# Attention and a gated spectral filter in one kernel: one load per ScalarE table, an earlier idle burst, split gates, and new orders for every engine

## The chip, the cores and the metric

One core of a Trainium2 chip runs the program. The metric is the device time of one execution in microseconds; lower is better. The engines are TensorE (PE), ScalarE (ACT), VectorE (DVE), GpSimd (POOL) and SyncE (SP, which issues most transfers). The profile gives starts and durations of the instructions of one execution.

## The reference

Eight batches, twelve heads, 448 positions, 64 elements to a head; float32 in and out.

```python
scores = scale * np.matmul(q, k.transpose(0, 1, 3, 2))
m = np.max(scores, axis=-1, keepdims=True)
e = np.exp(scores - m)
attn = e / (np.sum(e, axis=-1, keepdims=True) + np.exp(-m) + 1e-09)
x = np.matmul(attn, v)                     # then heads side by side: (8, 448, 768)
proj = x @ w_proj                          # 768 x 2304
x1, x2, x3 = proj[..., :D], proj[..., D:2*D], proj[..., 2*D:]
x2_conv = irfft(rfft(x2, axis=1) * rfft(filter_fft, axis=0))
out = (x1 * x2_conv * x3) @ w_out
```

## The kernel before, in words

Matrices are multiplied in bf16. The work of a batch has two parts.

**Attention** runs over six pairs of heads. For each pair the keys and queries are loaded, cast to bf16 and turned so that the head's elements lie across the partitions. PE makes four score tiles (`S`, t = 0 to 3; tile 0 holds the last 64 keys of both heads), ACT takes the exponential of each (`exps`, lines 852 and 858), PE multiplies by the values (`V`, line 878, with a column of ones that gives the sum), and DVE divides (`norm`). The result is turned again (`X`, line 975 for batch 0, by transfers for the others).

**The dense part** folds the turned result into even and odd parts along the sequence (`first`, `second`), projects it (`P`, line 1067, or `PS`, line 1089), takes the spectrum by matmuls with sines (`Z`), multiplies by the filter's spectrum on DVE, goes back (`I`), makes two gates (`G`, line 1189: six matmuls over the 768 inputs, `part` 0 copied by ACT, `part` 1 multiplied by it on DVE), and projects to the output (`O`, line 1003). Attention of the next batches is mixed with the dense part of the earlier ones on every engine.

**What sets the order.** Each step is given to a planner by `add(engine, cost, want, emit, need, make, take, give)`. `need` and `make` are the step's dependencies, `take` and `give` its buffers and PSUM banks. The tuple `plan.ORDER` has one rank for each `add` call, in the order of the calls; each engine emits its own steps strictly by rank. The planner also plays the steps through with the written costs, to choose PSUM banks and to put idle matmuls (line 1464) into gaps on PE near the start. An engine executes its steps in the written order and waits in place for what a step needs; SP's and POOL's transfers stand in the same queues as their other steps.

**The start.** `idle` is a zeroed tile and `spin` (line 1472) multiplies it 38 times, a burst of idle matmuls. `phases` and `sines` build the table of sines (DVE, then ACT at line 707); two one-column activations, `warm` with Exp (line 1479) and `warm` with Sin (line 1477), have no use but that of loading a function table. The compiler puts an ACT_TABLE_LOAD ahead of any activation whose function isn't in the table that is loaded. `staged(b)` loads batches 0 and 1 in float32 (`sk`, `sq`, `sv` for keys, queries, values of a pair; `rk`, `rv` for the last 64 positions), casts them (`ck`, `cq`, `cv`; pair 0's keys and queries on DVE, the rest on POOL) and turns them on PE (`T`, lines 530 to 539); later batches are turned by transposing transfers on SP. The weights come by POOL's queue: the filter, then w(0), w(1,0), w(1,1), w(2) and the output weights; w(1,0) and w(1,1) are the halves of the middle third of `w_proj`, which `P` uses.

**The end.** A check for very small denominators is read as a branch; the last output projections stand behind it.

## Time and profile before

| | us |
|---|---|
| median of 3 runs | 380.03 (379.71 to 380.31) |
| the profiled execution | 377.33 |
| its span, first to last instruction | 375.3 |
| PE busy, of the span | 358.9 |
| ACT, DVE, POOL busy | 265.3, 260.5, 113.8 |

The profiled execution is one execution, with a time of its own: its span and 2.0 us around it. Busy times are sums over one engine's instructions. In lists of instructions the columns are start, duration, engine, line, operation, output and inputs, count; in brackets stands how long the engine had been idle, and what ended that.

### The profile page before, as it was taken

The numbers are of one execution on the slowest core, as the hardware profiler recorded it, in microseconds if no ns is written. First come the engines' busy times: TensorE is split into PE (matmuls) and PEld (weight loads), VectorE is DVE, ScalarE is ACT, GpSimd is POOL, SyncE is SP. The second block draws the span as 40 slices with busy tenths as digits, with TensorE's granted clock in tenths as the row PEclk, the third lists the DMA queues.
The fourth block names the chain that finished last, engine by engine and source line by source line (L and its number), as shares of the span: only waits on it lengthen the run. The fifth ranks groups of instructions, "written<-read, shape, count | busy, mean of one in ns | idle before, by whom it ended". The sixth has DMA issues, their size and how long they took to land. (4 is left out here: it accounts for less than half of the span.)

```text
span 375.3 us, 9304 instructions
## 1 busy us (share of the span) xinstructions
PE 358.9 (96%) x3586; PEld 215.8 (58%) x3586; DVE 260.5 (69%) x676; ACT 265.3 (71%) x457; POOL 113.8 (30%) x240
## 2 busy tenths in 40 slices
PE   4899999999999999999899999999999999999985
PEld 4567675656665575555455556655555556555543
DVE  6389488865898556994498848684576936958570
ACT  5899967786877677677489477777788766436523
POOL 5765735142555441733272443120000000000000
PEclk9999999999999999999999999999999999999999
DMA  8999999999999999999999889796713054513304
GB/s 224 270 247 239 248 245 192 215 196 248 252 216 228 241 259 216 271 230 234 245 232 250 193 188 226 191 184 165 113 16 86 2 75 137 128 15 72 127 7 169
DMA packets 132019, 68.41 MB, mean 182 GB/s; under 512 B 88765, under 2 KB 128384, under 8 KB 131968
## 3 DMA queue, kind: packets, MB, share of 16 engines
q1 hardware_dynamic: 127248, 62.11, 73.6%
q0 software_dynamic: 4480, 5.41, 8.5%
q8 instruction: 29, 0.48, 0.5%
q10 hardware_dynamic: 240, 0.23, 0.2%
q14 instruction: 22, 0.18, 0.1%
HBM read 43.86 MB, written 11.01 MB: 146 GB/s over the span
## 5 line engine op out<-in xcount | busy, mean ns | idle before, releaser
L852 ACT ACTIVATE e<-psum 128x896 bf16<-128x896 f32 x144 | 126.8, 923 | 20.3 <-PE psum L839 18.0
L1189 PE MATMUL psum<-xT,wproj_bf 128*128 128x448 bf16 x576 | 121.8, 352 | 0.3 <-DVE kT L549 0.2
L1189 PEld LDWEIGHTS <-wproj_bf 128*128 128x128 bf16 x576 | 53.2, 97 | 46.4 <-issue 3.4
L1003 PE MATMUL psum<-wout_bf,yT 128*128 128x384 bf16 x288 | 52.8, 326 | 0.0
L878 PE MATMUL psum<-vn,e 128*128 128x65 bf16 x1152 | 46.9, 194 | 0.0
L878 PEld LDWEIGHTS <-e 128*128 128x128 bf16 x1152 | 41.6, 98 | 5.1 <-issue 0.8
L839 PE MATMUL psum<-qT,kT 64*128 64x448 bf16 x288 | 41.5, 355 | 1.4 <-DMA kT<-nat 0.9
L1157 DVE TENSOR_TENSOR t<-xs,hrs 113x768 bf16<-113x768 bf16 (+1 forms) x64 | 39.6, 641 | 4.3 <-ACT xs L1151 4.1
L1204 DVE TENSOR_TENSOR g<-x,psum 128x448 bf16<-128x448 bf16 x48 | 29.5, 615 | 17.3 <-PE psum L1189 14.2
L636 POOL CAST nat<-nat 112x512 bf16<-112x512 f32 x36 | 23.7, 666 | 49.6 <-DMA nat<-in_q_dram 47.6
L1089 PE MATMUL psum<-xf,wproj_bf 128*128 128x452 bf16 x180 | 38.6, 356 | 0.0
L1303 ACT COPY osb<-psum 128x384 f32<-128x384 f32 x56 | 25.5, 487 | 18.3 <-PE psum L1003 11.4
L1003 PEld LDWEIGHTS <-yT 128*128 128x128 bf16 x288 | 27.3, 98 | 18.6 <-issue 1.1
L1151 ACT CAST xs<-psum 113x384 bf16<-113x384 f32 (+1 forms) x64 | 29.0, 488 | 12.3 <-PE psum L1139 8.3
L1201 ACT CAST x<-psum 128x448 bf16<-128x448 f32 x48 | 25.7, 539 | 14.5 <-PE psum L1189 13.8
L893 DVE TENSOR_TENSOR xb<-psum,den 128x512 bf16<-128x512 f32 x48 | 33.2, 691 | 1.7
L858 ACT ACTIVATE er<-psum 128x448 bf16<-128x448 f32 x48 | 26.2, 549 | 11.2 <-PE psum L841 10.9
L1237 ACT CAST cr<-psum 128x452 bf16<-128x452 f32 x48 | 24.6, 545 | 7.9 <-PE psum L1228 5.8
L668 POOL CAST vn<-nat 128x192 bf16<-128x192 f32 x58 | 22.6, 416 | 24.9 <-PE psum L878 14.8
L891 DVE TENSOR_SCALAR den<-psum 128x8 f32<-128x8 f32 x48 | 7.8, 163 | 31.7 <-PE psum L878 26.4
L656 POOL CAST nat<-nat 128x384 bf16<-128x384 f32 x29 | 17.1, 594 | 32.5 <-DMA nat<-in_k_dram 31.6
L1067 PE MATMUL psum<-wproj_bf,xf 128*113 128x384 bf16 x144 | 26.6, 328 | 0.0
(130 smaller groups left out, 464.6 us busy)
## 6 DMA issues: line engine op xcount, KB each, us to landing
nat<-in_q_dram SPq DMA_DIRECT2D x47, 224.0 KB, 4.3
out_dram<-osb SPq DMA_DIRECT2D x24, 384.0 KB, 3.3
nat<-in_v_dram SPq DMA_DIRECT2D x41, 192.0 KB, 4.4
nat<-in_k_dram SPq DMA_DIRECT2D x41, 192.0 KB, 4.3
wproj_bf<-in_moe_w_proj_dram POOLq DMA_DIRECT2D x2, 1152.0 KB, 12.6
rests<-in_k_dram SPq DMA_DIRECT2D x8, 192.0 KB, 5.3
rests<-in_v_dram SPq DMA_DIRECT2D x8, 192.0 KB, 4.9
out_dram<-osb SPq DMA_DIRECT2D x8, 192.0 KB, 3.0
```

What stands on the lines that cost most here:

```text
L839: nc.tensor.matmul(sc[:, u, 0:S], kT[b % 2][c, hp, t, :], qT[b % 2][c, hp, :])
L852: nc.scalar.activation(to, of, AF.Exp, scale=SCALE)
L858: nc.scalar.activation(to, of, AF.Exp, scale=SCALE)
L878: nc.tensor.matmul(out_bank(u)[:, n, :], P["e"][1 + t][:, u * S + n * 128 : u * S + n * 128 + 128], vn[b % 2][:, hp, 4 * u + t, :], start= ...
L893: nc.vector.tensor_tensor(W["xb", b][:, hp].rearrange("p n (u d) -> p u n d", u=2), op[:, :, :, 0:DH], rec[:].unsqueeze(3).to_broadcast([1 ...
L1003: nc.tensor.matmul(ops[:n, :DCH], y[:, dt, 0:n], wout_bf[:, dt, ch * DCH : (ch + 1) * DCH], start=(dt == 0), stop=(dt == NDT - 1),)
L1067: nc.tensor.matmul(pps[:FQ, :DCH], W["xf", b][:, pg, kt, 0:FQ], wproj_bf[:, kt, D + ch * DCH : D + (ch + 1) * DCH], start=(kt == 0), stop= ...
L1089: nc.tensor.matmul(pps, wproj_bf[:, kt, D + dt * 128 : D + (dt + 1) * 128], W["xf", b][:, :, kt, 0:FQ], start=(kt == 0), stop=(kt == NDT - 1),
L1151: nc.scalar.copy(L["xs", par, ch][:K, pg % 2, :], L["Z", pg, ch][:K, :DCH])
L1157: nc.vector.tensor_tensor(t[:K], L["xs", par, ch][:K], h, op=ALU.mult)
L1189: nc.tensor.matmul(p[:, :S], wproj_bf[:, kt, 2 * part * D + dt * 128 : 2 * part * D + (dt + 1) * 128], xT()[:, kt, 0:S], start=(kt == 0), ...
L1204: nc.vector.tensor_tensor(g[:, dt, :], L["x1", dt], p[:, :S], op=ALU.mult)
```

## The change

Four edits, and a new tuple of ranks.

- The Exp warm-up makes a token `exp table`, the sines need `sine table`, and the exponentials of the first two head pairs need `exp table`; the three stand in that order in the new ranks too.
- The idle burst and the loads of the first keys come first by the new ranks.
- In batch 0, four gates are each given to the planner as two steps: the first four or five of the six matmuls (`G4`), which need only the first four or five turned pairs, and the rest.
- `plan.ORDER` has 2027 ranks in place of 2023, and nearly every rank differs.

```diff
+    AHEAD = {(0, 0): 4, (0, 1): 4, (1, 0): 5, (1, 1): 5}
...
-    plan.ORDER = (8, 2, 11, 33, 6, 13, 18, 29, ...)
+    plan.ORDER = (... 2027 ranks ...)
...
-  add("ACT", ..., lambda t=t: exps(t), need=[("S", i, t)] + ([] if i < 2 else ...),
+  add("ACT", ..., lambda t=t: exps(t), need=[("S", i, t)] + (["exp table"] if i < 2 else []) + ([] if i < 2 else ...),
...
-        def gate(dt, part, hy):
+        def gate(dt, part, hy, kts=range(NDT)):
             L["G", dt, part] = p = bank(hy)
-            for kt in range(NDT):
+            for kt in kts:
...
-            add("PE", 1.135, w, lambda: gate(dt, part, hy),
-                need=[("xT", b, h) for h in range(NHP)] + [("w", 2 * part, 0), ("w", 2 * part, 1)] + ...,
-                make=[("G", b), ("G", b, dt, part)], take=[hy])
+            k = AHEAD.get((dt, part)) if b == 0 and calm else None
+            ws = [("w", 2 * part, 0), ("w", 2 * part, 1)] + ...
+            if k:
+                add("PE", 0.19 * k, w - 1.0, lambda: gate(dt, part, hy, range(k)), need=[("xT", b, h) for h in range(k)] + ws,
+                    make=[("G4", b, dt, part)], take=[hy])
+                add("PE", 1.135 - 0.19 * k, w, lambda: gate(dt, part, hy, range(k, NDT)),
+                    need=[("xT", b, h) for h in range(k, NDT)] + [("G4", b, dt, part)], make=[("G", b), ("G", b, dt, part)])
+            else:
+                add("PE", 1.135, w, lambda: gate(dt, part, hy), ...)
...
-        add("ACT", 0.6, -19.0, sines, need=["phases"], make=["sines"])
-        add("ACT", 1.5, -16.0, lambda: nc.scalar.activation(warm, zero1, AF.Exp), need=["zero1", "sines"])
+        add("ACT", 0.6, -19.0, sines, need=["phases", "sine table"], make=["sines"])
+        add("ACT", 1.5, -16.0, lambda: nc.scalar.activation(warm, zero1, AF.Exp), need=["zero1", "sines"], make=["exp table"])
```

Sorted by rank, the two tuples give each engine these first steps (`T0q` turns the queries of pair 0, `T0` the last 64 keys; `S0.1` is score tile 1 of pair 0; `bps` and `rps` belong to the sines' tables, `ft` to them too; `half` is made by six small operations):

| engine | before | after |
|---|---|---|
| SP | sv2, sq1, rk, sv3, sk0, sk1, sv0, rv, sq2, sk2, sk4, sq3, sv1, sk3, sq4 | sk0, sk1, sq1, rk, sv0, sq2, sk2, sq3, rv, sv1, sk3, sq4, sk4, sv2, sv3 |
| DVE | row, zero1, half, phases, idle, cq0, zero ks, ft, qT0, ck0, rk cast | row, idle, phases, zero1, ck0, zero ks, cq0, half, qT0, rk cast, ft |
| ACT | load sq0, sines, warm Exp, warm Sin, kT0, exps 0.0, 0.1, 0.2, 0.3 | load sq0, warm Sin, sines, kT0, warm Exp, exps 0.1, 0.2, 0.0, 0.3 |
| PE | T0q, bps, burst, T(0), T0, S0.0, S0.1, T(1), S0.2, S0.3, S1.1 | burst, T0q, T(0), S0.1, T0, T(1), S0.2, bps, S0.3, S0.0, rps, S1.1 |
| POOL | count, ones, ones, pads, ident, cq1, rk cast, ck1, filter, cv0, ck2, rv cast, cq2, cv3 | count, ident, pads, ones, cq1, ck1, rk cast, cv0, filter, rv cast, cq2, ck2, cv1, cq3, ck3, cv3, ck4, cq4 |

Later on POOL, before: ck7, ck8, cq8, w(1,1), cv8, cq9, ck9, cq10, cv9, w(2). After: ck7, cv6, cv7, ck8, w(1,1), cq8, rv cast, cq9, ones, w(2), ck9, ck10, cq10. On PE, the gates and projections of batch 0 begin like this. Before: T(7), G(0,0), P(2,0), P(1,0), S, T(8), P(0,0). After: G4(0,0), hps, T(7), rest of G(0,0), P(1,0), P(2,0), S, P(3,0), T(8), P(0,0).

## The prediction

> **What bounds the kernel now.** I read the page's engine line first, then busy time in stretches, then the first 12 us engine by engine, then PE's waits.

> ```profile
> span 375.3 us, 9304 instructions
> PE 358.9 (96%) x3586; PEld 215.8 (58%) x3586; DVE 260.5 (69%) x676; ACT 265.3 (71%) x457; POOL 113.8 (30%) x240
> ```

> PE idles 375.3 - 358.9 = 16.4 us in all. In stretches (PE busy and PEclk, DMA share, GB/s last):

> ```profile
> 12.00:36.00 24.00, 22.08 (x346) 15.65 (x345) 18.64 (x48) 22.56 (x36) 15.32 (x30) 1.00 1.16 246
> 36.00:60.00 24.00, 23.67 (x248) 15.53 (x248) 17.27 (x48) 19.23 (x34) 12.40 (x26) 1.00 1.17 242
> 60.00:120.00 60.00, 60.00 (x626) 36.85 (x623) 49.05 (x123) 46.42 (x78) 25.46 (x48) 1.00 1.08 222
> 120.00:200.00 80.00, 76.72 (x776) 45.43 (x775) 55.79 (x133) 56.70 (x99) 35.30 (x75) 1.00 1.08 242
> 200.00:360.00 160.00, 160.00 (x1477) 91.17 (x1474) 110.05 (x297) 109.50 (x196) 17.40 (x34) 1.00 0.55 122
> ```

> From 36 us on PE is the bound: 0.3 us idle to 60, none to 120, 3.3 to 200, none to 360. Nothing useful can be taken out of it; the end moves only by the time at which PE's real work begins, plus changes in those gaps. From 12 to 36 ACT, busy 22.6 of 24 us, sets the pace with the exponentials of batch 0. Before 12, two lists (start, length, engine, what):

> ```profile
> 5.91 4.03 PE L1472 MATMUL psum<-idle 128*128 128x128 bf16 x38
> 9.79 0.33 PE L532 MATMUL psum<-ident_bf,ldm 128*128 128x128 bf16 x3
> ...
> 10.49 0.36 PE L841 MATMUL psum<-qT,kT 128*128 128x448 bf16 x1
> ```

> ```profile
> 5.40 1.28 ACT L1479 ACT_TABLE_LOAD   x1
> 6.69 0.20 ACT L1479 ACTIVATE warm<-zero 128x1 f32<-128x1 f32 x1
> 6.91 1.28 ACT L1477 ACT_TABLE_LOAD   x1
> ...
> 10.15 0.48 ACT L551 COPY kT<-psum 128x384 bf16<-128x384 bf16 x1 [1.74 <-PE psum L532]
> 10.65 1.28 ACT L858 ACT_TABLE_LOAD   x1
> 11.94 0.54 ACT L858 ACTIVATE er<-psum 128x448 bf16<-128x448 f32 x1
> ```

> The first keys were cast at 7.17 to 7.53, but their turn waits behind the idle burst until 9.79; then the first exponential waits for a fourth table load, since the sine warm-up (L1477) had thrown the exponential's table out. The chain is burst, turn, copy, table, exponential at 11.94. I did not expect the table loads at 5.40 and 6.91 to cost anything: ACT then waits 1.74 us for PE anyway.

> The last reading is POOL's list around 38 us:

> ```profile
> 38.29 0.59 POOL L491 CAST ldm<-nat 128x384 bf16<-128x384 f32 x1 [3.17 <-DMA nat<-in_k_dram]
> 38.96 0.74 POOL L497 CAST ldm<-nat 112x512 bf16<-112x512 f32 x1
> 39.65 0.82 POOL L817 DMA_DIRECT2D wproj_bf<-in_moe_w_proj_dram  x1
> ```

> The keys of head pair 8 were asked for at about 24.95 and landed at 38.2, with the DMA share at 1.16 throughout: this stretch is full of transfers. Behind that cast stands the load of the second half of the middle projection, w(1,1), which lands 9.6 us later, at 49.25; its first matmul starts at 49.33. DMA and PE arrive together there.

> **The change, part by part.**

> *Tables.* Two of four loads go, 2 x 1.28 = 2.57 us of ACT. Only the one at 10.65 was on the path: 1.28. In the new order the exponential's load stands behind the copy of the first keys and still shows in part. [...]

> *Burst and first keys.* The burst needs only its zeroed operand, now the second DVE instruction: 1.43 (end of the row cast) + 0.11 gives 1.55, and 3.88 us of burst (5.91 to 9.79) ends it at 5.45, beside the loads. Keys of pair 0 go first on SP; the first SP load of before landed 3.7 us after 0.75, so 4.45. Then DVE in its new order: cast of keys 0.36, zeroing 0.38, cast of queries 0.36 to 5.55, the six weight operations 1.03 (1.47 to 2.50 in before) to 6.6, query copy 0.61 to 7.2. PE turns queries and keys 5.6 to 6.25 while this runs; ACT copies the keys (0.48) to 6.75, loads the table (1.28) to 8.05, warms (0.20) to 8.25. The first score, after the query copy, ends at 7.6. First exponential at about 8.25 instead of 11.94: 3.7 us sooner. Two waits lie behind it: the cast of the values of pair 3 now stands ahead of the casts of pair 4 on POOL, and the 15th SP load of before was cast at 17.83 on arrival, so pair 4's turn comes near 18.9 and ACT, there at 18.4, waits 0.5 to 1.0. Before, ACT lost 1.3 us in the same chain (19.82 us from 11.94 to 31.76, against 24 exponentials at 2.85 per pair = 17.1, 0.9 mirror, 0.45 one spectrum copy). These cancel; 3.7 stays.

> *Gates ahead.* 18 matmuls of 0.19 (six take 1.14, 57.00 to 58.15) = 3.4 us in parts of four or five. Reading the new order, only the first part (0.76) passes anything large, the turn of pair 7; the others stand within two steps of their rest. It can fill at most the 0.5 us of idle matmuls and the 0.1 gap at 34.9 to 35.5, when its weights are there (w0 is issued at 20.39 and lands by 33.0). I take 0, for what follows decides; ends 0 and 0.6.

> *What is late next.* Every load that pair 8 needs stands in the same DMA stream. Its keys move from 29th to 28th on SP (values of pair 8 go behind); the stretch moves a load in 0.78 us (from 38.2 to 42.1 for five), so they land at 37.4. Cast to 37.9, w(1,1) issued to 38.8, now ahead of the cast of pair 8's queries, which ends at 39.4; so the turn of pair 8 is at 39.4. In before it was at 40.77, and the new order has one projection (0.98, 41.21 to 42.19) more in front of it: that work was done at 41.8. Gain there: 2.4. w(1,1) lands at 38.0 + 9.6 = 47.6, for a matmul that now has one turn (0.43, 44.62 to 45.05) and one score (0.19) more ahead of it (49.95 in before): again 2.4. Turn of pair 9 waits for a cast behind w(2)'s issue, 41.75 against an arrival of 41.4: 0.35 more. Of 3.7 us, **2.0** come through. Ends: 1.2 (keys no sooner than 38.2) and 3.7 (transfers follow the earlier start, since SP too waits in places for casts: 2.9 us of its waits to 60 are for L491).

> *The order from 60 us on.* No row shows it. The distances that matter, counted in PE work at the rows' pace (0.98 a projection, 1.14 a gate, 0.39 a product of values), are much the same: between the last attention product of a batch and its folded projection stand 8.7 to 12 us of PE work, against 9.5 to 12.3 before; between still projection and spectrum 5.2 to 16.3 against 5.1 to 16.0. I take 0. Ends: all 3.3 us of the gaps at 120 to 200 go, or as much and a little more, 4, is added. The last DVE steps and the twelve last projections are the same in number: 0.

> Sum, on the profiled execution: 377.33 - 2.0 = 375.3 (span 373.3). The median of the runs, 380.03, lies 2.70 above that execution; I carry this over: 378.0.

> **Rivals.**

> *The whole start comes through.* Speaks for it: SP waits for casts, which come sooner. Against: DMA share 1.16. 380.03 - 3.7 = 376.3. A condition is PE's clock. The 38 idle matmuls took 3.88 us, 102 ns each, seven fillers right after them 56 each (0.55 less the first's 0.22, over six): the burst runs at about half rate, though PEclk shows 1.00 in every stretch. After the earlier burst PE has some 1.7 us of work from 5.5 to 9. [...]

> *Slower: the SP queue from 60 to 200 us.* It holds loads, transposing transfers and stores in one written order; a transposing transfer occupied it for 1.2 to 2.6 us, and two of the waits end on one:

> ```profile
> PE psum L839 <- DMA kT<-nat: 0.9, 1, 0.9
> PE psum L1139 <- DMA x<-ldm: 0.7, 1, 0.7
> ```

> In the new order several of them changed places (the first one of x moved ahead of the queries' of pair 12). If one is held by a late product, all loads behind it are. It decides once such waits add over 2.8 us to these 1.6; two misplaced ones, 2 x 2.0, give 380.03 - 2.0 + 4.0 = 382.0. Against it: 5 to 12 us of PE work lie between.

> *No difference.* Gain at the start 2.0, one such wait of 2.0 later: 380.0.

> *The change doesn't do what it says.* A third table load would show, placed in front of the copy of a projection; the copies and the scaling of before ran without one after 11.94. Little: 379.

> **Numbers.** Forecast (377.0 to 379.2) 0.46; whole start, with or without some of the gaps at 120 to 200, 0.20; no difference 0.10; slower 0.20; not as said 0.04, half of it within what can't be told. A measurement tells 0.2% (0.76 us) from no change. So faster 0.68, same 0.12, slower 0.20. Range: 375.2 (3.7 at the start and 1.1 of the gaps) to 381.6 (the start's 2.0 and 3.6 lost).

> **What would show it.** Two table loads; burst near 1.6; first exponential near 8.3; ACT's last exponential of batch 0 near 28; cast of pair 8's keys near 37.5 after a wait for DMA; turn of pair 8 near 39.4; first matmul of w(1,1) near 47.6; PE gaps of about 3 us at 120 to 200. Wrong if pair 8 is turned before 38 (then 376.3), if scores before 12 us take double, or if PE waits over 6 us between 60 and 360.

## The result, and the profile after

The changed kernel takes 381.70 us (median of 7 runs, 380.88 to 382.30), the kernel before 379.95 (379.46 to 380.83) on the same chip: ratio 1.0044 [1.0029, 1.0059], slower by 0.4% in this set (a second set, on another chip, does not repeat it; see below). The forecast was 378.0, with a range up to 381.6, and faster at 0.68. Ratios leave out executions more than 1.5% above the fastest of their kernel, and the means further below those over 388 us.

The profiled execution took 382.25, 0.5 above the median; the one of before lay 2.6 below its own. So the two spans, 380.5 and 375.3, are further apart (5.2) than the medians of the kernels are (1.75).

The engine line of the page after, first: 2.2 us less of ACT, for the two table loads (2.57) that are gone, and 4.4 us more of PE for seven more instructions. PE is idle for 380.5 - 363.3 = 17.2 us, against 16.4 before: the earlier start has not taken idle time away.

```profile
span 380.5 us, 9321 instructions
PE 363.3 (95%) x3593; PEld 218.5 (57%) x3593; DVE 261.0 (69%) x676; ACT 263.1 (69%) x455; POOL 111.8 (29%) x240
```

The start, from the lists of PE and of ACT (start, length, engine, line, what; in brackets the idle time before and what ended it):

```profile
1.56 4.23 PE L1480 MATMUL psum<-idle 128*128 128x128 bf16 x38 [1.56 <-DVE idle L1468]
...
6.52 0.48 ACT L552 COPY kT<-psum 128x384 bf16<-128x384 bf16 x1 [1.74 <-PE psum L533]
7.02 1.28 ACT L1487 ACT_TABLE_LOAD   x1
8.31 0.20 ACT L1487 ACTIVATE warm<-zero 128x1 f32<-128x1 f32 x1
8.42 0.90 ACT L853 ACTIVATE e<-psum 128x896 bf16<-128x896 f32 x1
```

The first exponential starts at 8.42 (11.94 before): the 3.5 us were gained. They last through batch 0 and go after it: the end of ACT's 24th exponential, the last of batch 0, is at 28.36 (31.76 before), of its 28th at 40.74 (41.69), of its 40th at 59.74 (57.44). In stretches (length, then PE, PEld, DVE, ACT, POOL busy; granted clock of PE, DMA share, GB/s):

```profile
12.00:36.00 24.00, 22.68 (x348) 15.70 (x345) 18.90 (x54) 22.19 (x37) 13.69 (x30) 1.00 1.16 239
36.00:60.00 24.00, 20.36 (x213) 13.94 (x214) 12.43 (x32) 14.99 (x26) 10.99 (x24) 0.93 1.14 228
60.00:120.00 60.00, 59.42 (x617) 36.38 (x615) 47.57 (x117) 44.60 (x78) 25.22 (x51) 1.00 1.06 224
120.00:200.00 80.00, 76.89 (x733) 44.49 (x731) 56.14 (x135) 55.79 (x97) 37.23 (x74) 0.98 1.05 233
200.00:360.00 160.00, 159.96 (x1509) 92.03 (x1506) 110.48 (x294) 111.91 (x199) 17.93 (x37) 1.00 0.58 130
```

From 36 to 60 PE is idle for 3.6 us, against 0.3 before, issues 213 matmuls instead of 248, and its mean clock is 0.93. The same stretch in PE's list, projections only (L1068), and then PE busy, clock, DMA share and GB/s in steps of 2 us:

```profile
37.36 2.13 PE L1068 MATMUL psum<-wproj_bf,xf 128*113 128x384 bf16 x12 [1.60 <-DMA wproj_bf<-in_moe_w_proj_dram]
...
51.22 3.82 PE L1068 MATMUL psum<-wproj_bf,xf 128*113 128x384 bf16 x12 [2.25 <-DMA wproj_bf<-in_moe_w_proj_dram]
```

```profile
50.00:52.00 2.00, 0.78 (x3) 0.80 1.13 227
52.00:54.00 2.00, 2.00 (x8) 0.50 1.17 207
54.00:56.00 2.00, 2.00 (x13) 0.84 1.19 230
```

PE waits for w(1,0) until 37.36 and for w(1,1) until 51.22. After the second wait the same twelve matmuls that took 2.13 us take 3.82: PE runs at half its clock (0.50 from 52 to 54 us). POOL's list shows why w(1,1) is late:

```profile
38.32 0.64 POOL L505 CAST vn<-nat 128x192 bf16<-128x192 f32 x2 [3.29 <-DMA nat<-in_v_dram]
39.34 0.51 POOL L492 CAST ldm<-nat 128x384 bf16<-128x384 f32 x1 [0.38 <-DMA nat<-in_k_dram]
39.79 0.82 POOL L818 DMA_DIRECT2D wproj_bf<-in_moe_w_proj_dram  x1
```

POOL waits 3.29 us for the values of pair 7, whose cast now stands in front, then casts the keys of pair 8 at 39.34 (38.29 before). So w(1,1) is issued at 39.79, as before (39.65), and needs 11.4 us instead of 9.6. PE has another wait of this kind, of 2.13 us up to 186.17, ahead of batch 3's second gate group (released by ACT, x transposed by a transfer that was issued at 178.60); the clock falls to 0.5 behind it too. In the profile of before the clock is 1.00 up to 374.8.

Two theories. A: a pause of TensorE of about 2 us (2.25 and 2.13 here) can let its clock fall to half for a few us, and the new order has more such pauses. B: until about 200 us the stream of transfers (DMA share 1.03 to 1.11 in each 50 us) decides when PE's work can run, so an earlier start only makes PE wait longer for weights. Rivals: the start is worth its 3.5 us and the new order loses them elsewhere; or the split gates do harm.

### The profile page after: what moved, and what is told of

Its sections match the earlier page's. It is cut to its first block, busy times and chain, and to the rows that moved or that the text cites. A ratio compares the mean times of both kernels' runs of the same rounds, so it can differ in the third digit from the quotient of the medians.

```text
span 380.5 us, 9321 instructions
## 1 busy us (share of the span) xinstructions
PE 363.3 (95%) x3593; PEld 218.5 (57%) x3593; DVE 261.0 (69%) x676; ACT 263.1 (69%) x455; POOL 111.8 (29%) x240
## 5 line engine op out<-in xcount | busy, mean ns | idle before, releaser
L1190 PE MATMUL psum<-xT,wproj_bf 128*128 128x448 bf16 x576 | 123.3, 355 | 0.2
L1190 PEld LDWEIGHTS <-wproj_bf 128*128 128x128 bf16 x576 | 54.3, 98 | 47.4 <-issue 4.6
L879 PE MATMUL psum<-vn,e 128*128 128x65 bf16 x1152 | 47.9, 194 | 0.0
L1158 DVE TENSOR_TENSOR t<-xs,hrs 113x768 bf16<-113x768 bf16 (+1 forms) x64 | 37.1, 601 | 4.7 <-ACT xs L1152 4.4
L1205 DVE TENSOR_TENSOR g<-x,psum 128x448 bf16<-128x448 bf16 x48 | 29.4, 615 | 14.3 <-PE psum L1190 11.1
L1311 ACT COPY osb<-psum 128x384 f32<-128x384 f32 x56 | 25.5, 488 | 16.3 <-PE psum L1004 9.6
L859 ACT ACTIVATE er<-psum 128x448 bf16<-128x448 f32 x48 | 26.3, 551 | 12.8 <-PE psum L842 11.9
L1068 PE MATMUL psum<-wproj_bf,xf 128*113 128x384 bf16 x144 | 28.3, 342 | 3.9 <-DMA wproj_bf<-in_moe_w_proj_dram 3.9
L669 POOL CAST vn<-nat 128x192 bf16<-128x192 f32 x58 | 20.9, 389 | 32.7 <-DMA nat<-in_v_dram 19.6
L1090 PEld LDWEIGHTS <-wproj_bf 128*128 128x128 bf16 x180 | 16.5, 96 | 16.7 <-issue 1.5
```

Source lines behind the costliest of these rows:

```text
L859: nc.scalar.activation(to, of, AF.Exp, scale=SCALE)
L879: nc.tensor.matmul(out_bank(u)[:, n, :], P["e"][1 + t][:, u * S + n * 128 : u * S + n * 128 + 128], vn[b % 2][:, hp, 4 * u + t, :], start= ...
L1068: nc.tensor.matmul(pps[:FQ, :DCH], W["xf", b][:, pg, kt, 0:FQ], wproj_bf[:, kt, D + ch * DCH : D + (ch + 1) * DCH], start=(kt == 0), stop= ...
L1090: nc.tensor.matmul(pps, wproj_bf[:, kt, D + dt * 128 : D + (dt + 1) * 128], W["xf", b][:, :, kt, 0:FQ], start=(kt == 0), stop=(kt == NDT - 1),
L1158: nc.vector.tensor_tensor(t[:K], L["xs", par, ch][:K], h, op=ALU.mult)
L1190: nc.tensor.matmul(p[:, :S], wproj_bf[:, kt, 2 * part * D + dt * 128 : 2 * part * D + (dt + 1) * 128], xT()[:, kt, 0:S], start=(kt == 0), ...
```

## The experiments

Below, *falls* of a run are (1 - its mean granted clock) x span / 1.71; 1.71 us is half of one low stretch of 3.41 us (shown in the next experiment). In nine of the thirteen profiles of these kernels one more low stretch, near the end, adds up to 0.64 to this count; in the profiles of before and after it begins at 374.8 and 378.9, and PE is busy for 0.00 us in it. Over 228 runs of all kernels, a run with one fall more than others of its kernel and chip is longer by 1.23 us (standard error 0.14): less than 1.71; why, no run shows.

**Pauses alone.** A kernel of nothing but matmuls, with pauses set by copies of VectorE:

```diff
+ for n in (900, 1100, ... 3100):          # twice over
+     44 to 60 matmuls 128x512   # the first reads gate
+     nc.vector.tensor_copy(gate[:, 0:n], ps[:, 0:n])
```

> Not the computation: only matmuls of 128 x 512 into one bank, in 25 stretches of 9 to 13 us, and between them 24 pauses of TensorE, each set by one copy of VectorE out of PSUM whose width goes from 900 to 3100 columns in twelve steps, twice over (estimate from the copies in the traces: pauses of 1.2 to 3.6 us); the output is zeros. Its total time says nothing. Theory A (a pause of about 2 us or more can let the clock fall to half for one window of 3.4 us, counted from a clock that runs by itself): no half rate after pauses under 1.7 us, in some of those of 1.8 to 3 us and in all the longest, each time for 3.3 to 3.5 us, and the starts of the half-rate stretches lie whole multiples of 3.4 us apart. Rival 1 (the length of the pause alone decides, counted from its own start): one sharp limit, the same in both turns. Rival 2 (the fall in the kernel comes from something else, as heat or transfers): no half rate after any pause.

Half rate follows 8 of the 24 pauses, for 3.41 us, twice for 6.83. They start at 113.57, 130.64, 161.36, 178.43, 260.35, 304.72, 335.44, 352.51: all whole multiples of 3.413 apart, within 0.02. So the falls of this run keep to a grid of windows of 3.413 us, and the length of the pause alone doesn't decide. Two pauses of 2.65 us, in PE's list, and the windows on that grid (PE busy, clock):

```profile
114.13 0.61 PE L75 MATMUL ps<-idle,gate 128*128 128x512 bf16 x1 [2.65 <-DVE gate L76]
...
289.38 0.39 PE L75 MATMUL ps<-idle,gate 128*128 128x512 bf16 x1 [2.65 <-DVE gate L76]
```

```profile
110.16:113.57 3.41, 1.32 (x7) 1.00 0.00 0
113.57:116.98 3.41, 2.85 (x7) 0.50 0.00 0
116.98:120.40 3.42, 3.42 (x17) 1.00 0.00 0
```

The first pause leaves 2.10 us idle in one window, and the next window runs at 0.50. The second, just as long, is cut by a window's edge into 0.92 and 1.72, and nothing falls. Pauses of 3.06 and 3.07 us (1.22 and 1.84; 1.45 and 1.61) do nothing, one of 2.23 us within a window does. No window at full rate with up to 1.88 us idle was followed by a fall, every one with 2.10 or more was. Once low, the windows with 0.90 and 1.18 us idle were followed by another low one, that with 0.56 by full rate. In seven profiles of the kernels here ten falls stand behind windows with 1.83 to 2.61 us idle, and windows with up to 1.75 were followed by none; each lasts 3.41 or 3.42 us, and two in one profile lie whole multiples of 3.413 apart. The least idle time ahead of a fall is thus 1.83 us in the kernels and 2.10 with pauses alone, where 1.84 and 1.88 us had none (matmul ends are modelled). Rivals 1 and 2 fall.

The first fall begins at 51.22 and 50.98 in the two profiles of the changed kernel, and at 30.21 and 30.04 in the two of the kernel with w(1,1) earlier (below): in two executions of one kernel, on two chips, the windows lay differently against the program, by 0.24 and 0.17 us. That the same pause can fall in one run and not in another is an estimate from this. Of 18 runs of the changed kernel 12 had a mean clock of 0.996 or less, which the stretch at the end alone gave in no profile, of 93 of the kernel before 40.

**Pause at w(1,1) filled.**

```diff
+ if (b, pg, ch) == (0, 2, 1):
+     for _ in range(40): nc.tensor.matmul(pps[:, 0:128], idle, idle)
```

> The changed kernel with 40 idle matmuls (2.2 us at 56 ns) in front of the first projection that reads w(1,1), in the projection's own bank, where PE stood 2.25 us. Theory A (the wait lets PE's clock fall, and the 12 matmuls behind it took 3.82 us where 2.13 is usual): the granted clock stays at 1.0 from 50 to 56 us, those matmuls take 2.1 us, and the time falls by about 1.7 us, from 381.7 to 380.0 (ratio to before 1.000). Rival (the slow matmuls are slow for another reason, such as transfers into the same memory): they stay at 3.8 us and the time is unchanged at 381.7, ratio 1.004.

379.52, ratio 0.9973 [0.9940, 1.0005]; falls 0.72 per run. Nothing useful was added or moved. The time equals that of the kernel before; on another chip, below, so does that of the changed kernel, so the time alone shows little. The profile shows the effect. In PE's list of this kernel the twelve matmuls take 2.11 us again:

```profile
47.88 2.40 PE L1070 MATMUL psum<-idle 128*128 128x128 bf16 x40
50.11 2.11 PE L1072 MATMUL psum<-wproj_bf,xf 128*113 128x384 bf16 x12
```

A holds at this place: the clock stays at 1.00, where it fell in both profiles of the changed kernel.

**Pause at batch 3's gates filled.** The same with 36 idle matmuls ahead of the first spectrum product that waited at 186.

> The changed kernel with 36 idle matmuls (2.0 us) in front of the first spectrum matmul of batch 3, where PE stood 2.13 us at 184 us. Theory A (clock): the granted clock stays at 1.0 from 186 to 191 us (0.50 in the changed kernel) and the time falls by about 1.9 us to 379.8, ratio 0.9997. Rival (the wait alone costs, the clock comes back in work that has slack): unchanged, 381.7, ratio 1.004.

383.34, ratio 1.0080 [1.0047, 1.0114]; falls 1.21 per run, no fewer. The expectation was missed. In its profile a wait of 1.31 us for the same release comes ahead of the idle matmuls, which then run to 185.67: they were queued behind the wait, not inside it, and cost their full 2 us there. But this profiled execution, 379.82, was the fastest of nine; why the others are slower and why the falls stayed was not settled.

**Burst 3.7 us longer.** The start of the changed kernel is given away.

```diff
- SPIN = 38
+ SPIN = 104
```

> The changed kernel with 104 idle matmuls in the burst in place of 38, so that the first turn on PE and the first exponential start about 3.7 us later, at about 12.1, as in the kernel before. Theory B (the stream of transfers up to w(1,1) sets the time, and the earlier start only makes PE wait): the waits for w(1,0) (1.6 us) and w(1,1) (2.25 us) shrink by what the start loses, and the time stays within 0.7 us of 381.7, or is less where a shorter wait keeps the clock. Rival (the start is worth what it moves, and the loss is made elsewhere): 381.7 + 3.7 = 385.4, ratio 1.014.

381.79, ratio 1.0042 [1.0012, 1.0071], as the changed kernel. The first score exponential starts at 11.25, and yet (PE's list):

```profile
49.85 2.16 PE L1068 MATMUL psum<-wproj_bf,xf 128*113 128x384 bf16 x12 [0.42 <-DMA wproj_bf<-in_moe_w_proj_dram]
```

2.8 us later at the start, this matmul is 1.4 us earlier than in the changed kernel's first profile, and 0.4 earlier than in its second (50.25). B: the earlier start buys nothing here. The transfers did not follow it. Up to 38 us (PE busy, clock, DMA share, GB/s) the kernel before, the changed one and this one have:

```profile
0.00:38.00 38.00, 30.90 (x433) 1.00 1.09 245
0.00:38.00 38.00, 32.85 (x445) 1.00 1.09 234
0.00:38.00 38.00, 34.53 (x507) 1.00 1.09 240
```

The DMA share is the same, and with the earlier start no more bytes came by then than without it. Corrected for falls, the means of the two kernels differ by 0.6 (standard error about 0.7, and the chips differ), so a worth of more than 2 us is excluded, a smaller one not.

**Tables alone.** The kernel before with the change's table steps and ACT's first steps in its order:

```diff
-  sines, need=["phases"]
+  sines, need=["phases", "sine table"]
-  ... AF.Exp), need=["zero1", "sines"])
+  ... AF.Exp), need=["zero1", "sines"], make=["exp table"])
```

> The kernel before with one edit of the change alone: the sine warm-up ahead of the sines, the exponential's behind the copy of the first keys, so that two of four table loads go. The first exponential starts near 11.1 in place of 11.94, since its table is still loaded behind the copy at 10.15 unless it fits ahead. Theory B (transfers): w(1,0) lands at 37.9 all the same and the time changes by less than 0.5 us, ratio 0.999 to 1.001. Rival (ACT's chain sets the time): up to 1.3 us less, 378.7, ratio 0.9966.

380.34, ratio 0.9989 [0.9957, 1.0022]: no difference. Two loads instead of four, but the exponential starts at 11.70 instead of 11.94, for the second load still follows the key copy; the forecast had 1.28 of this on the path. Its profile had a fall too, at 135.13, behind a pause of 1.8 us for a transposing transfer.

**The changed kernel once more, on the chip of the next three.**

> The changed kernel itself, as the yardstick of this set. All theories: ratio to the kernel before 1.0029 to 1.0059, as measured first. Theory A (a wait of about 2 us lets TensorE's clock fall): in the profile the twelve matmuls of the second projection column of pairs 8 to 11 take 2.1 us where the granted clock stays whole and 3 to 4 us where the wait ahead of them was about 2 us. Rival (the new order is slower everywhere by a little): they take 2.1 us and the loss is spread from 60 to 360 us.

381.27, ratio 0.9987 [0.9944, 1.0031]: on this chip the two can't be told apart. Its runs spread from 376.92 to 384.79, besides one of 597.48. The profiled one took 378.54, with one fall, after the wait for w(1,1) (2.28 us); at batch 3's gates it paused 1.49 us and nothing fell. Over both sets the means are 381.0 for the changed kernel (18 runs) and 380.5 for the one before (93 runs, three chips): a difference of 0.5, with a standard error of 0.5. That the change costs time at all is shown by the first set only; that it gains nothing, by both.

**w(1,1) issued earlier**, ahead of two casts (one, the expectation says). POOL's order:

```diff
  cast keys 7, cast values 6,
+ load w(1,1),
  cast values 7, cast keys 8,
- load w(1,1),
  cast queries 8
```

> The second half of batch 0's third projection weight is issued one cast earlier on GpSimd (ahead of the cast of value tile 7). Theory B (the landing of this weight decides): issue at about 35 instead of 39.8, landing at 46 to 47, the wait of 2.25 us ahead of its first matmul gone or under 0.5 us, the keys of pair 8 about 1 us later; time 379 or below, ratio 0.993 to 0.999. Rival (the DMA stream only shares itself out anew): what this weight gains the keys and values of pair 8 lose, the work ahead of it ends 2 us later, and the ratio stays at 1.003 to 1.006.

379.52, ratio 0.9953 [0.9922, 0.9984]: faster. Issued at 35.70, the weight lands by 46.9 (11.2 us), and its matmuls wait for nothing (PE's list):

```profile
50.42 2.11 PE L1068 MATMUL psum<-wproj_bf,xf 128*113 128x384 bf16 x12
```

But they start at 50.42 all the same, since the profile shows a pause of 2.00 us at 29.14, for keys cast by POOL, and a fall behind it (clock 0.55 and 0.59 from 30 to 34). A second fall stands behind a pause of 2.06 us at batch 3's gates. So in this profile the transfers hold back what stands ahead.

> The changed kernel with the second half of batch 0's third projection weight ahead of the cast of value tile 7, once more. Theory B: ratio 0.992 to 0.998 as in the first run, so that the earlier start is worth 1 to 3 us once this weight comes in time. Rival (the first result was chance): 1.001 to 1.006.

379.29, ratio 0.9990 [0.9956, 1.0023] on another chip: less than expected, with overlapping intervals. Over both (24 runs) the mean is 379.5 with 1.02 falls, against 381.0 with 1.18 for the changed kernel (18 runs) and 380.5 with 0.57 for the kernel before (93, three chips). That it beats the changed kernel by about 1.5 is likely (standard error 0.6). Against the kernel before the means differ by 1.0 (standard error 0.4), but the second set alone doesn't show a gain.

**The same move in the kernel before** (ahead of the keys of pair 8, two casts).

> The kernel before with the second half of batch 0's third projection weight issued one cast earlier on GpSimd (ahead of the cast of the keys of pair 8, which waits 3.2 us for its load). Theory B: the weight lands 3 to 4 us sooner, but here the start is the late one, so the work ahead of this weight ends at about 50 as it did (49.95) and nothing is gained: ratio 0.998 to 1.002. Rival (the landing of this weight sets the pace in the kernel before too, or the other transfers that it puts back do): ratio 0.995 or lower, or 1.003 or higher.

379.73, ratio 1.0000 [0.9969, 1.0032], as B expected. Issued at 35.34 instead of 39.65, its first matmul is 0.46 earlier (48.87 against 49.33). The four loads of `w_proj` needed 11.0 to 13.6 us here (9.6 to 13.4 before).

**w(2) issued later**, behind five casts more (two, the expectation says).

> The weight of batch 1's first projection is issued two casts later on GpSimd, no longer close behind the second half of batch 0's third projection weight. Theory C (the two loads share the queues, and the first lands late for it): landing 9.6 us after its issue, as in the kernel before, instead of 11.4, the wait ahead of its first matmul 0.5 us instead of 2.25, ratio 0.997 to 1.001. Rival (the late landing comes from the other transfers under way, of the keys and of the rows for the gates): landing still 11 us or more after the issue, and ratio 1.003 to 1.006.

382.09, ratio 1.0036 [1.0004, 1.0068]. w(1,1) needed about 11.1 us even so: theory C falls. With the change's order this load needed 10.7 to 11.9 us in every profile, with that of before 9.6, 10.1 with the tables alone, and at least 11.0 where it was issued earlier; what lengthens it was not settled. Two other waits came up (2.61 for w(1,0), 2.01 for w(2)), and 1.60 falls per run.

**Gates whole.**

```diff
- AHEAD = {(0, 0): 4, (0, 1): 4, (1, 0): 5, (1, 1): 5}
+ AHEAD = {}
```

> The gates of batch 0 are not split: all their matmuls come where the second parts stand, and nothing of them is moved ahead. Theory B: moving them ahead fills time in which TensorE would otherwise wait for weights, so without it TensorE waits about 2 us longer at the first projection column of pairs 8 to 11 and is later by their 2 to 3 us behind it: ratio 1.006 to 1.010. Rival (the gates moved ahead stand in the way of the work that follows and fill nothing): ratio 1.000 to 1.003.

380.17, ratio 0.9984 [0.9952, 1.0017]; on the same chip the changed kernel had 0.9987. The waits for weights are there as before (0.87 and 2.14). Moving the gates ahead is worth nothing that shows; the ratio lies below what either theory gave.

**A version against both causes:** w(1,1) earlier and short fillers.

```diff
+ 10 idle matmuls ahead of the turn of the keys of pair 6
+ 16 idle matmuls ahead of batch 3's second gate group
```

> The same, and idle matmuls in the two places where this kernel's profile had pauses of 2 us: 10 ahead of the transposes of the keys of pair 6 (about 0.6 us) and 16 ahead of the first gate matmul of batch 3's second group (0.9 us), which cut pauses of 2.0 and 2.1 us to 1.4 and 1.2. Theory A: fewer runs with a lowered mean clock (below 0.997 in 1 run of 4 or fewer, against 5 of 12 without them), 0.5 to 1.5 us faster than without them, ratio 0.988 to 0.996. Rival (the idle matmuls cost what they take and the clock falls elsewhere): 0 to 1.5 us slower than without them.

378.90, ratio 0.9991 [0.9961, 1.0022]; falls 0.66 per run (1.12 without the fillers on this chip), and 4 of 12 runs have a mean clock under 0.997 (8 without). This is in the right direction, but 0.4 faster is within the noise, and the ratio does not show that this version beats the kernel before. At the gates its profile has no wait ahead of the fillers, so there they only cost their 0.9 us.

Its profile shows where a gain at 48 us goes. PE's matmuls of w(1,1) start at 47.96 without a wait or a fall; in the changed kernel's second profile PE was there at the same time, waited 2.28 and lost 1.71 more to the clock (half of one low stretch). Yet the spans are 376.9 and 376.8. In stretches (PE busy, clock, DMA share, GB/s), this kernel:

```profile
48.00:60.00 12.00, 10.05 (x92) 1.00 1.08 250
60.00:100.00 40.00, 39.72 (x436) 1.00 1.06 210
100.00:120.00 20.00, 18.00 (x171) 1.00 1.04 228
```

and the changed one:

```profile
48.00:60.00 12.00, 9.75 (x82) 0.86 1.14 224
60.00:100.00 40.00, 40.00 (x421) 1.00 1.08 212
100.00:120.00 20.00, 19.45 (x204) 1.00 0.99 241
```

Of the 4.0 saved, 1.95 come back before 60 as a pause for keys cast by POOL, 0.28 to 100, and 1.45 more idle time than in the changed kernel from 100 to 120. By the start of the same score matmul, this kernel is ahead by 3.7 us at 54, by 1.8 at 62 and by 1.1 at 100, behind by 0.5 at 116, and level from 220 on: PE does not wait for this weight, so it waits for the next things.

## Why the prediction was wrong

*Tables, burst and first keys: right.* Two loads; burst from 1.56 to about 5.6 (5.45); first exponential 8.42 (8.25). The load's length was 1.28 both times, and the next activation started 0.01 behind it (7.02 + 1.28, 8.31; before, 10.65 + 1.28, 11.94). ACT's last exponential of batch 0 ended at 28.36, as forecast (28). Of 3.7 us at the start, 3.4 were there at that point. The half rate that was feared for the scores behind an early burst did not come: two took 0.36, as before; only the two turns right behind the burst were slower (0.58 and 0.53 instead of 0.36 and 0.33).

*Gates ahead: right at 0*, by the runs with whole gates.

*What is late next: this step failed*, in three terms. It let 2.0 of the 3.7 us come through; the runs show none that can be told from noise. First, the keys of pair 8 were to land at 37.4, one place earlier on SP at 0.78 us a place. They landed at 39.2 in the first profile and at 38.2 in the second (38.15 before); pair 8 was turned at 40.93 and 39.87 (39.4 forecast). w(1,1) was issued at 39.79, and in the kernels that keep this order at 38.79 to 39.79, where 38.0 was forecast. SP's list shows when the keys were asked for:

```profile
23.35 4.93 SPq L470 DMA_DIRECT2D nat<-in_v_dram  x1
28.32 1.80 SPq L470 DMA_DIRECT2D nat<-in_k_dram  x1
```

One load of values held SP for 4.93 us, and the keys went out at 28.32 instead of 24.95. Whether this hold cost anything is not shown: 18 loads that SP issued from 9.88 to 41.99 landed in the order of issue (15.9 to 51.4), and the keys came, at 39.2, 1.0 us behind the values in front of them (issued at 23.35, landed at 38.25). Being one place earlier on SP moved nothing. Second, the time that w(1,1) takes to land, 9.6, was carried over from one execution of another order; with the new one it was 10.7 to 11.9. So 47.6 became 51.2 in the first profile and 50.2 in the second, while PE's work ahead of this weight was done at 48.97 and 47.97. Of the 3.6 and 2.6 us by which it came late, this term is 1.8 in each. Third, w(1,0) was left out of the sum: it took 16.1 us from its issue at 21.10, and PE waited 1.60 for it in the first profile, though not in the second.

*The clock.* The prediction weighed PE's clock for the burst alone. The pauses that mattered were those that the earlier start itself makes: PE arrives sooner at weights that don't (2.25 and 2.28 us ahead of w(1,1), then 0.50). At 1.18 falls per run against 0.57, and 1.23 us each, falls are worth 0.8 us, and the whole difference of the means is 0.5 (standard error 0.5). In the first set (1.43 falls) they are 1.1 of 1.75, if the kernel before had 0.57 there too, which is not on record; the rest is within the noise of the means.

*"2.0 come through"*: next to none did. Waits moved from 0 to 12 us to the places behind, and the rivals, which priced a wait at its length, had no price for the fall of the clock. The rival "no difference" (380.0) came nearest in mechanism; "slower" was right in sign, but put the cause on SP from 60 to 200. There only one such wait was found (2.13 at 186, against 0.7 and 0.5 of before), and with its fall it is worth some 2, an estimate. The forecast's 1.2 to 2.6 us for a transposing transfer was read too low: from 60 to 200 single ones held SP for up to 3.87 us in before.

*The order from 60 on at 0*: gaps at 120 to 200 were 3.1 (3.3 before), 0.6 at 60 to 120 (0): right in this profile but for the fall. No run changed this part of the order alone, so what it is worth by itself stays open.

*Median over execution, 2.70*: a term that varies. The execution of before had no fall and took 377.33, that of after had two and took 382.25; of 93 runs of before 53 have none. But these 53 take 379.6 in the mean, so the profiled execution was 2.3 below even those; why is open.

## What to carry to other kernels

Before crediting an earlier start, follow it to the next operand that comes by DMA and ask whether that operand's issue moves too; where the DMA share is as high as here (1.03 to 1.11 in each 50 us to 200), don't count on it. Price a wait of TensorE, where TensorE is the bound, at its length and, if it is about as long as those that fell here, at some 1.2 to 1.7 us more (1.23 over the runs; 1.71 is half of one low stretch), with a chance: with pauses alone the clock fell behind 8 of the 16 of 2.02 to 3.48 us, and behind none of the eight of 1.19 to 1.82. Judge changes of under 1% by many runs and their mean clocks, not by one profile of each.
